# Two additions of the output tail moved to GpSimd, and their stores one step later, in an attention and spectral-mix kernel

## The chip, the cores and the metric

The kernel runs on one core of a Trainium2 chip. The metric is device time in microseconds (us); lower is better. The core's engines run side by side, each with its own instruction queue: TensorE (PE; its weight loads are PEld), VectorE (DVE), ScalarE (ACT), GpSimd (POOL) and SyncE (SP), which here only issues transfers. Sixteen DMA engines move data between HBM and the on-chip memory. TensorE writes its results to PSUM, eight banks of accumulators.

## The reference

Attention with a local mask for half of the heads and a strided mask for the other half gives x, 8 batches of 576 tokens by 512 channels. Then a spectral mix, and an output layer with a residual:

```python
    X = np.fft.rfft(x, axis=1)
    Yr = np.einsum('bmd,mde->bme', Xr, w_r) - np.einsum('bmd,mde->bme', Xi, w_i)
    Yi = np.einsum('bmd,mde->bme', Xr, w_i) + np.einsum('bmd,mde->bme', Xi, w_r)
    y = np.fft.irfft(Y, n=S, axis=1)
    u = x + y
    return (u + np.maximum(u @ w_ch, 0.0)).astype(np.float32)
```

The first 64 frequencies ("modes") are mixed, each with its own two 512 x 512 matrices. What matters for the change is the last line: the output is u = x + y plus the relu of v = u @ w_ch.

## The kernel before, in words

The kernel has three stages. The first computes the attention, batch by batch, and its Fourier transform over the tokens. The second runs over the 64 modes in two halves of the input channels and streams in the weights (fp16 on chip) through GpSimd's DMA queue; the chip works on x @ w_ch and on spectra that are already whole in between. The third, the tail, is where the change lies.

Because the inverse transform is linear, u and v are sums of a part that is known early (x, and x @ w_ch, with the contributions of the first three groups of sixteen modes already added to them by `renew` during the second stage; they are kept in fp16 as `xos`/`xoh` and `v0s`/`v0h`) and the contribution of the last group. The tail adds that last contribution, takes the relu, adds and stores. It runs over 18 items (`items`, from line 973). Items 0 to 15 are 128 tokens of two batches each: 128 partitions by 2 x 512 values in fp32, 512 KB. Items 16 and 17 are the last 64 tokens of four batches each, again 512 KB.

Order of work is written out by hand; each engine runs its instructions in the order in which the program issues them. For each item k the program issues:

- `v_early(k)`, line 984: two matmuls with the identity put the kept v into a pair of PSUM banks (L987);
- `u_early(k)`, line 989: two matmuls with the identity put the kept x into another pair (L992);
- `new_rows(k, ...)`, line 994: two matmuls (four for items 16 and 17) add the last group's rows, once for v from the spectra `zzs`, once for u from `yys` (L1001). They use 32 rows of the array each;
- `v_done(k)`, line 1008: ScalarE writes the relu of v into a tile `rl` (L1013);
- `u_done(k)`, line 1015: VectorE adds u from PSUM and `rl` into the output tile `osb` (L1020), and SyncE issues the store (L1028). For items 16 and 17 four stores of 128 KB go out, two by SyncE and two by ScalarE (L1031).

The loop from line 1065 makes step k of v's first half for item k and the second half of u for item k - 1: in one step TensorE runs `v_early(k)`, `u_early(k-1)`, the rows of v for k, and the rows of u for k - 1; then come ScalarE's relu of k, VectorE's add for k - 1 and its store. Before step 8, four more matmuls (`spec_z(3, 1, held)`) and a ScalarE copy make the spectra `zzs[1]` of the second four batches.

Buffers: PSUM pool "p" has three pairs of banks, taken in turn by v of every item, by u of the even items, and once by `held`; pool "u" has one pair, for u of the odd items. `osb` comes from a pool of five buffers (NWBUF, line 27), so item k takes the buffer of item k - 5 once its store has landed. `rl` has two pairs of buffers.

Of the kernel before, what the change touches and what calls it, by code (L numbers as in the profile page):

```python
# [10 lines left out]
FP = mybir.dt.float32  # L11
F16 = mybir.dt.float16
AluOp = mybir.AluOpType
# [5 lines left out]
DM = 512  # L19
# [37 lines left out]
def kernel(  # L57
# [10 lines left out]
    nc = tc.nc  # L68
# [17 lines left out]
    def psum(kind, half=False, pair=False):  # L86
        if pair:
            return pss[kind].tile([128, 2, 512], FP, tag=kind, name=kind)
        if half:
            return pss[kind].tile([128, 1024], F16, tag=kind, name=kind)  # L90
        return pss[kind].tile([128, 512], FP, tag=kind, name=kind)
# [39 lines left out]
    pw = ctx.enter_context(tc.tile_pool(name="pw", bufs=NWBUF))  # L131
# [118 lines left out]
    def act_copy(out, in_):  # L250
        nc.scalar.activation(out=out, in_=in_, func=ACTF.Copy)  # L251
# [445 lines left out]
    def out_cols(t):  # L697
        if t < 4:
            return ds(256 * (t % 2) + 128 * (t // 2), 128)
        return ds(512, 64)  # L700

    v0s, xos = {}, {}
# [165 lines left out]
    xoh = [ptr.tile([128, DM], F16, name=f"xoh{i}") for i in range(4)]  # L868
    zzs = [ptr.tile([128, DM], F16, name=f"zz{i}") for i in range(B)]
    yys = [ptr.tile([128, DM], F16, name=f"yy{i}") for i in range(B)]  # L870
# [31 lines left out]
    A3 = cs["cFl"].rearrange("p a t m -> p (a t m)")[:, 0:S]  # L902
# [64 lines left out]
    for n, i in enumerate([3, 5, 7] + list(range(8, 21))):  # L967
        b, t = n // 2, n % 2 * 2
# [4 lines left out]
    items = []  # L973
# [6 lines left out]
    def own(item, kept, half):  # L980
        bs, t = item
        return [kept[b][:, t] for b in bs] if t < 4 else [half[b // 2] for b in bs[::2]]

    def v_early(k):
        vps[k] = psum("p", pair=True)
        for j, r in enumerate(own(items[k], v0s, v0h)):
            nc.tensor.matmul(vps[k][:, j], idn, r, start=True, stop=False)  # L987

    def u_early(k):
        ups[k] = psum(("p", "u")[k % 2], pair=True)  # L990
        for j, r in enumerate(own(items[k], xos, xoh)):
            nc.tensor.matmul(ups[k][:, j], idn, r, start=True, stop=False)  # L992

    def new_rows(k, acc, spectra):
        bs, t = items[k]
        for j, b in enumerate(bs):
            q = ds(32 * (b % 4), 32)
            o, cols = acc[:, j % 2], out_cols(t)
            if t == 4:
                o = acc[ds(64 * (b % 2), 64), j // 2]  # L1000
            nc.tensor.matmul(  # L1001
                o, A3[q, cols], spectra[b // 4][q], start=False, stop=True
            )

    def pieces(k):
        return [slice(0, 1), slice(1, 2)] if k == 0 else [slice(0, 2)]

    def v_done(k):
# [3 lines left out]
        for j in pieces(k):  # L1012
            nc.scalar.activation(out=rls[k][:, j], in_=vp[:, j], func=ACTF.Relu)  # L1013

    def u_done(k):
        bs, t = items[k]
        up, rl = ups.pop(k), rls.pop(k)
        osb = pw.tile([128, 2, DM], FP, tag="w", name="osb")
        for j in pieces(k):
            nc.vector.tensor_tensor(  # L1020
                out=osb[:, j], in0=up[:, j], in1=rl[:, j], op=AluOp.add
            )
            if t < 4:
                rows = out[:, ds(128 * (t - t % 2), 256), :].rearrange(
                    "b (p i) e -> p b i e", i=2
                )
                own_b = slice(bs[0] + j.start, bs[0] + j.stop)
                nc.sync.dma_start(rows[:, own_b, t % 2], osb[:, j])  # L1028
        if t == 4:
            for b in bs:  # L1030
                (nc.scalar if b % 2 else nc.sync).dma_start(  # L1031
                    out[b, ds(512, 64), :], osb[ds(64 * (b % 2), 64), b // 2 % 2, :]
                )

    flush()
    rest = [(0, m) for m in range(SPLIT1, NM)] + [(1, m) for m in range(SPLIT0, NM)]
    late[22] = [lambda: v_early(0), lambda: v_early(1), lambda: u_early(0)]
    for i, (slot, m) in enumerate(rest):
        mode(slot, m)
# [16 lines left out]
    for k in range(2):  # L1056
        new_rows(k, vps[k], zzs)
    for k in range(2):
        v_done(k)
    for k in range(2):  # L1060
        if k:
            u_early(k)
        new_rows(k, ups[k], yys)
        u_done(k)
    for k in range(2, LAST + 2):
        if k == 8:
            held = psum("p", pair=True)[:, 0]
            spec_z(3, 1, held)
            act_copy(zzs[1], held)
        if k <= LAST:  # L1070
            v_early(k)
        if k > 2:
            u_early(k - 1)
        if k <= LAST:
            new_rows(k, vps[k], zzs)
        if k > 2:
            new_rows(k - 1, ups[k - 1], yys)
        if k <= LAST:
            v_done(k)
        if k > 2:  # L1080
            u_done(k - 1)
# [31 lines left out]
```

## Time and profile before

| | |
|---|---|
| median of three runs | 428.08 us (427.69 to 428.46) |
| profiled execution: span, first to last instruction | 426.7 us |
| profiled execution: device time of its own | not given by the page |
| busy PE, DVE, ACT, POOL | 346.4, 234.7, 218.3, 110.7 us |
| mean granted TensorE clock | 0.926 |
| data moved by the core's DMA engines | 91.62 MB, mean 215 GB/s |
| written to HBM | 9.44 MB |
| store of an item (512 KB): issues, median time to landing | 15, 3.4 us |

The profile is one execution. Its times are us from the span's start. "L987" is line 987 of the kernel. A line of the timeline gives the start, the duration, the engine, the line, the operation, out<-in with partitions x elements and type, how many, and in brackets how long the engine had been idle and what it waited for. SPq and ACTq are the queues that issue transfers. DMA share is the mean busy share of the sixteen DMA engines. The chain that ended last follows the work back from the last instruction, at each step to what released it.

### The profile page before, as it was taken

What the parts mean: (1) busy time and instruction counts of PE and PEld (TensorE: products, weight loads), DVE (VectorE), ACT (ScalarE), POOL (GpSimd) and SP (SyncE); (2) the same over time, 40 slices, a digit from 0 to 9 for tenths busy, and PEclk for the clock granted to TensorE, in tenths of its full rate; (3) what the DMA queues carried; (4) which work ended last, traced back from release to release, by engine and by line L of the source; (5) the groups of instructions that cost most, each with busy time, mean ns of one, the idle gap of its engine ahead of it and who ended that gap; (6) DMA issues with size and microseconds to landing.
All of it is one profiled execution on the core that took longest, in us unless ns stands there. A gap on an engine that the chain in (4) does not pass through costs nothing.

```text
span 426.7 us, 9768 instructions
## 1 busy us (share of the span) xinstructions
PE 346.4 (81%) x4167; PEld 208.2 (49%) x4167; DVE 234.7 (55%) x466; ACT 218.3 (51%) x390; POOL 110.7 (26%) x196
## 2 busy tenths in 40 slices
PE   2977878769999698889768788878788867889993
PEld 2866767554656365566433344435444423445330
DVE  3788778851355154356113246746676354655884
ACT  1687678643656356556642235423442444443872
POOL 8332333322423222222222322222232222210000
PEclk9999899967999689999995889989999979989997
DMA  8999999999999999999999999999999999995698
GB/s 150 210 212 212 213 213 213 211 211 211 214 213 213 213 213 215 212 214 215 210 214 211 213 214 213 210 213 215 212 213 214 213 213 214 214 212 105 244 355 287
DMA packets 30938, 91.62 MB, mean 215 GB/s; under 512 B 4464, under 2 KB 5232, under 8 KB 30896
## 3 DMA queue, kind: packets, MB, share of 16 engines
q0 software_dynamic: 25168, 81.28, 96.2%
q1 hardware_dynamic: 4976, 9.13, 5.9%
q10 hardware_dynamic: 752, 0.61, 0.5%
q8 instruction: 32, 0.52, 0.5%
q14 instruction: 10, 0.08, 0.0%
HBM read 162.83 MB, written 9.44 MB: 404 GB/s over the span
## 4 chain that ended last, share of the span: by engine, by line
DMA 47%; PE 29%; DVE 14%; ACT 5%; issue 3%; DVEq 0%; POOL 0%; ACTq 0%; POOLq 0%
DMA wt<-in_moe_w_i_dram 38%; DMA wt<-in_moe_w_r_dram 7%; PE y L597 5%; DVE xb L241 3%; DVE kz L283 3%; PE p L987 2%; ACT X L251 2%; PE sc L532 2%; PE tp L413 2%; PE sc L459 1%; PE p L1001 1%; PE y L532 1%; PE p L760 1%; DVE yy L752 1%; DVE rec L240 1%
## 5 line engine op out<-in xcount | busy, mean ns | idle before, releaser
L597 PE MATMUL y<-wt,X 128*32 128x512 f16 (+1 forms) x448 | 70.9, 430 | 20.1 <-DMA wt<-in_moe_w_i_dram 20.1
L186 POOL DMA_DIRECT2D wt<-in_moe_w_r_dram x59 | 34.7, 588 | 126.4 <-PE y L597 56.3
L186 POOL DMA_DIRECT2D wt<-in_moe_w_i_dram x60 | 35.4, 590 | 68.3 <-DMA wt<-in_moe_w_i_dram 44.4
L597 PEld LDWEIGHTS <-X 128*32 128x32 f16 (+1 forms) x448 | 28.1, 140 | 39.4 <-DMA wt<-in_moe_w_i_dram 18.6
L727 DVE COPY xo<-tp 128x512 f16<-128x512 f16 x32 | 22.1, 691 | 36.8 <-PE tp L725 36.8
L726 ACT ACTIVATE v<-sc 128x512 f16<-128x512 f32 x32 | 19.1, 597 | 44.2 <-PE sc L717 44.2
L717 PE MATMUL sc<-w_cp,xT 128*128 128x512 f16 x128 | 36.9, 410 | 1.9 <-DVE xT L690 1.9
L489 ACT ACTIVATE PL<-sc 128x480 f16<-128x480 f32 (+1 forms) x48 | 27.0, 578 | 21.3 <-PE sc L475 21.0
L241 DVE TENSOR_TENSOR xb<-av,rec 90x256 f16<-90x256 f32 (+2 forms) x80 | 36.0, 450 | 2.8
L240 DVE RECIPROCAL rec<-av 90x4 f32<-90x4 f32 (+2 forms) x80 | 14.6, 183 | 39.3 <-PE av L504 28.2
L251 ACT ACTIVATE yr<-y 128x512 f16<-128x512 f32 x28 | 16.7, 597 | 36.8 <-PE y L597 35.6
L961 DVE TENSOR_TENSOR xo<-p,xo 128x1024 f16<-128x1024 f32 x16 | 19.6, 1225 | 21.7 <-PE p L760 21.7
L420 DVE COPY qT<-tp 128x576 f16<-128x576 f16 x16 | 11.9, 752 | 34.7 <-PE tp L413 34.7
L251 ACT ACTIVATE v<-p 128x1024 f16<-128x1024 f32 x16 | 16.4, 1023 | 23.1 <-PE p L760 23.1
L378 ACT ACTIVATE PL<-sc 90x360 f16<-90x360 f32 (+1 forms) x48 | 22.7, 490 | 7.0 <-PE sc L371 6.4
L251 ACT ACTIVATE v<-tp 128x640 f16<-128x640 f16 (+1 forms) x24 | 19.0, 807 | 11.8 <-PE tp L447 9.3
L413 PE MATMUL tp<-cI_s,ring 64*64 64x64 f16 x864 | 22.4, 197 | 2.7 <-DVE qT L420 2.4
L459 PE MATMUL sc<-cMl_s,cI_s 128*128 128x480 f16 (+1 forms) x48 | 19.4, 405 | 4.5 <-ACT PL L489 2.9
L276 PE MATMUL tp<-cI_s,ring 72*128 72x72 f16 x256 | 15.4, 207 | 8.7 <-DMA ring<-in_v_dram 7.1
L413 PEld LDWEIGHTS <-ring 64*64 64x64 f16 x864 | 17.5, 110 | 9.4 <-issue 5.4
L251 ACT ACTIVATE kz<-tp 64x360 f16<-64x360 f16 (+1 forms) x32 | 18.9, 592 | 6.2 <-PE tp L413 5.2
L1013 ACT ACTIVATE rl<-p 128x1024 f32<-128x1024 f32 (+1 forms) x19 | 18.4, 979 | 5.7 <-PE p L1001 3.1
(142 smaller groups left out, 737.9 us busy)
## 6 DMA issues: line engine op xcount, KB each, us to landing
wt<-in_moe_w_i_dram POOLq DMA_DIRECT2D x60, 512.0 KB, 18.8
wt<-in_moe_w_r_dram POOLq DMA_DIRECT2D x59, 512.0 KB, 17.7
out_dram<-osb SPq DMA_DIRECT2D x15, 512.0 KB, 3.4
ring<-in_v_dram POOLq DMA_DIRECT2D x8, 288.0 KB, 13.4
ring<-in_q_dram POOLq DMA_DIRECT2D x8, 288.0 KB, 13.6
ring<-in_k_dram POOLq DMA_DIRECT2D x8, 288.0 KB, 13.1
ring<-in_v_dram POOLq DMA_DIRECT2D x3, 512.0 KB, 14.8
ring<-in_q_dram POOLq DMA_DIRECT2D x3, 512.0 KB, 14.8
```

The lines of the kernel that those rows point to most:

```text
L186: nc.gpsimd.dma_start(dst, rows)
L241: nc.vector.tensor_tensor(out=dst, in0=val.rearrange("p h (q c) -> p h c q", c=4), in1=rec[0:n, 0:pieces] .to_broadcast((n, pieces, 64)) . ...
L251: nc.scalar.activation(out=out, in_=in_, func=ACTF.Copy)
L378: nc.scalar.activation(out=PS[0:n, ds(POFF[t], 4 * n)], in_=scp[0:n, 0 : 4 * n], func=ACTF.Exp, scale=SCALE,)
L413: nc.tensor.transpose(tp[ds(64 * hp, 64), ds(64 * i, 64)], qn[ds(64 * hp, 64), ds(64 * (9 * g + i), 64)], idn[ds(64 * hp, 64), ds(64 * hp, ...
L459: nc.tensor.matmul(scp[:, 0 : n * times].rearrange("p (h x) -> p h x", h=times), idn, mask_rows("cMl", n, times), start=True, stop=False,)
L489: nc.scalar.activation(out=dst, in_=src, func=ACTF.Exp, scale=SCALE)
L597: nc.tensor.matmul(yp[ds(a, 32), :], Xh[half][pr, c].rearrange("p b r (h m) -> p (b r h) m", h=2)[:, :, mm % 32], wt[pr, XC[c], :], start= ...
L717: nc.tensor.matmul(vp, xT[:, ch], w_chs["cp"][:, ch, :], start=(ch == 0), stop=(ch == 3),)
L726: nc.scalar.activation(out=v0, in_=vp, func=ACTF.Copy)
L727: nc.vector.tensor_copy(out=xo.rearrange("p (h q c) -> p h q c", h=2, c=4), in_=tp[:, 0:512].rearrange("p (h c q) -> p h q c", h=2, c=4),)
L961: nc.vector.tensor_tensor(out=xo, in0=up[:, 0:n], in1=xo, op=AluOp.add)
```

## The change

Items 2, 6, 8, 12 and 14 (`XADD`) leave out `u_early`: x isn't put into PSUM by TensorE. The first row matmul opens the accumulation instead (`start=fresh`). VectorE adds the relu as before, and then GpSimd adds x, in two instructions of 128 x 512, from the kept fp16 tile onto the fp32 output tile.

Items 4 and 10 (`RADD`) keep `u_early`, but VectorE's add is left out: ScalarE copies u from PSUM to `osb`, and GpSimd adds the relu in one instruction of 128 x 1024.

The store of these seven items isn't issued in their own `u_done` but in that of the next item, behind that item's own store. The store's code is the same, in a function of its own.

```diff
+    XADD = (2, 6, 8, 12, 14)
+    RADD = (4, 10)
+
     def u_early(k):
         ups[k] = psum(("p", "u")[k % 2], pair=True)
+        if k in XADD:
+            return
         for j, r in enumerate(own(items[k], xos, xoh)):
             nc.tensor.matmul(ups[k][:, j], idn, r, start=True, stop=False)
 
     def new_rows(k, acc, spectra):
         bs, t = items[k]
+        fresh = spectra is yys and k in XADD
...
             nc.tensor.matmul(
-                o, A3[q, cols], spectra[b // 4][q], start=False, stop=True
+                o, A3[q, cols], spectra[b // 4][q], start=fresh, stop=True
             )
...
+    stores = {}
+
+    def store(k):
+        if k not in stores:
+            return
+        osb = stores.pop(k)
...
     def u_done(k):
-        bs, t = items[k]
         up, rl = ups.pop(k), rls.pop(k)
-        osb = pw.tile([128, 2, DM], FP, tag="w", name="osb")
+        osb = stores[k] = pw.tile([128, 2, DM], FP, tag="w", name="osb")
+        if k in RADD:
+            act_copy(osb, up)
+            nc.gpsimd.tensor_tensor(out=osb, in0=osb, in1=rl, op=AluOp.add)
+            return
         for j in pieces(k):
             nc.vector.tensor_tensor(
                 out=osb[:, j], in0=up[:, j], in1=rl[:, j], op=AluOp.add
             )
...
+        if k in XADD:
+            for j, r in enumerate(own(items[k], xos, xoh)):
+                nc.gpsimd.tensor_tensor(out=osb[:, j], in0=osb[:, j], in1=r, op=AluOp.add)
+            return
+        store(k)
+        store(k - 1)
```

## The prediction

> **What bounds the kernel now.** I read the two dies' table first (one core, clock 0.926, 426.7 us), then the page's slices, the chain that ended last, the tail's stretches, and the timeline and DMA issues of the tail. The chain puts 47% of the span on weight loads. They end at 391.6 us; the change lies wholly behind them, in the tail of 18 items from 396.7 us on. There the chain names TensorE:
>
> ```profile
> 414.90 0.43 PE p L992 x2
> 415.33 0.33 PE p L1001 x4
> 415.66 0.54 PE p L987 x2
> 416.20 0.43 PE u L992 x2
> 416.63 0.34 PE p L1001 x4
> ...
> 418.92 0.83 DVE osb L1020
> 419.75 0.08 issue
> 419.83 1.44 DVEq L1108
> ```
>
> A step is 0.54 + 0.43 + 0.33 = 1.30 us of TensorE: two matmuls of v, two of x, four of spectral rows. But the stretches (columns: busy us of PE, PEld, DVE, ACT, POOL; clock, DMA share, GB/s) show a second full resource:
>
> ```profile
> 401.00:408.00 7.00, 6.86 (x42) 2.24 (x42) 5.49 (x5) 5.01 (x7) 0.00 (x0) 1.00 1.00 374
> 408.20:409.00 0.80, 0.80 (x8) 0.20 (x5) 0.80 (x1) 0.74 (x1) 0.00 (x0) 1.00 0.19 72
> 409.00:421.00 12.00, 10.69 (x72) 3.23 (x68) 10.89 (x10) 8.19 (x8) 0.00 (x0) 1.00 1.02 380
> 422.00:425.00 3.00, 0.00 (x0) 0.00 (x0) 0.00 (x0) 0.00 (x0) 0.00 (x0) 0.50 0.88 307
> ```
>
> DMA share is 1.00 and 1.02 at 374 to 380 GB/s. An item is 512 KB, so its store takes 524,288 B / 380 GB/s = 1.38 us, and items come every 1.30 us: the stores are already slower than TensorE. Only the gap around 408.5 us, after the extra matmuls of step 8, lets the queue run dry. The timeline and the issues give the other prices:
>
> ```profile
> 404.16 1.02 ACT L1013 ACTIVATE rl<-p 128x1024 f32<-128x1024 f32 x1 [0.27 <-PE p L1001]
> 404.25 1.23 DVE L1020 TENSOR_TENSOR osb<-p,rl 128x1024 f32<-128x1024 f32 x1
> 405.13 0.60 ACT L251 ACTIVATE zz<-p 128x512 f16<-128x512 f32 x1
> 406.72 1.23 DVE L1020 TENSOR_TENSOR osb<-u,rl 128x1024 f32<-128x1024 f32 x1 [1.24 <-PE u L1001]
> ...
> 420.06 1.22 DVE L1020 TENSOR_TENSOR osb<-u,rl 128x1024 f32<-128x1024 f32 x1
> 420.17 2.44 SPq L1031 DMA_DIRECT2D out_dram<-osb  x4
> ```
>
> ```profile
> 7.19 1.16 POOL L329 COPY PL<-cT_s 128x576 f16<-128x576 f16 x1
> ```
>
> ACT's relu is 1.02 us, VectorE's add 1.23, and GpSimd's one arithmetic row of size is 1.16 us for 576 elements. A store issued at 407.97 has its first packet at 408.86 and has landed 2.8 us after issue: 0.9 to the first packet, 1.38 of data, 0.5 to land.
>
> **Part 1: x leaves TensorE for five items.** Ten L992 matmuls go, 0.43 us a pair: 5 x 0.43 = 2.15 us of TensorE. Taken alone that is the gain, if nothing else bound. The row matmuls that now open the accumulation cost nothing extra: the same four stand in the step. But VectorE still adds relu (1.23 us, with starts at best 1.14 apart: 418.92 to 420.06), so a pair of items falls to 2.3, not 2.17 us, while its stores need 2.76 us. The saved time has nowhere to go.
>
> **Part 2: GpSimd.** Two adds of 512 elements per x item, one of 1024 per relu item; none is in the trace. From below, VectorE's 1.2 ns an element: 1.2 us an item. Nearest, the copy's 2.02 ns an element: 2.1 us. From above, one copy's time for each of the two inputs: 4.1 us. I take 2.25, near the copy row with a little for the second input; up to 2.6 us, two steps, GpSimd keeps up. POOL's queue is otherwise empty: its last weight load is issued at 382.3.
> The Trainium skill (GPSIMD Engine Reference, sections 3.1 and 4.1) speaks against the change: elementwise work belongs on VectorE, GpSimd taking 4497 ns for 2048 fp32 against 2293. By that an item's adds are an estimated 2.25 us; by the copy row they are 2.1, and the end is the same either way.
>
> **Part 3: relu of items 4 and 10.** VectorE loses two adds (2.46 us); ACT gains two 1.02 us copies, each behind the next item's relu. ACT idles 0.27 us a step, so a copy leaves it about 0.75 us late for the next relu; TensorE's buffers absorb part of it. It eats what item 2 saved: the copy of item 4 ends near 403.3, relu 6 near 404.35 (ended at 403.88 before), relu 7 near 405.4, the copy of zz[1] near 406.0, and VectorE adds item 7 at 406.7, as before.
>
> **Part 4: the order of stores.** On SP each of the seven even stores is put behind the odd one: 3, 2, 5, 4, ... 15, 14, and waits there for GpSimd; behind it in SP's queue wait the next pair's stores and, at the end, SP's half of 16 and 17. The number of SP issues (0.37 us each) is unchanged. I walk both kernels by the same prices (issue + 0.9, then 1.38 in order).
>
> Before: item 2 (issue 400.32) starts at 401.22; items 2 to 6 are out at 401.22 + 6.90 = 408.12; item 7 (407.97) starts at 408.87; items 7 to 15 are out at 408.87 + 12.42 = 421.29.
>
> After: item 1 is unchanged. Relu 2 ends at 398.64 (ACT is busy with four relus from 395.53), relu 3 at 399.65; TensorE's step 4 cannot start before 398.64 and ends at 399.95; item 3's add runs 400.0 to 401.24, issue 401.29, first packet 402.19 where item 2's stood at 401.22: the queue loses 0.97 us. Item 3 out 403.57; item 2 (add to 399.95, GpSimd to 402.2) 404.95; item 5 406.33; item 4 (copy to 403.3, GpSimd to 405.6, first packet 406.54) 407.92, 0.21 lost; item 7 (issue 408.01, packet 408.91) 410.29, with item 6, long added by VectorE, behind it: 0.99 lost, where the gap was 0.75 before. Then 6, 9, 8, 11, 10, 13, 12, 15, 14 without gap: 410.29 + 12.42 = 422.71. That is 0.97 + 0.21 + 0.24 = 1.42 us later than 421.29.
>
> **Buffers.** Five output buffers: item k waits for the store of k-5. Item 6, out at 411.67, lands at 412.2, and item 11's add waits 0.5 us for it; that is covered, since its store still arrives (414.4) before 414.43. Item 17 waits for item 12 (419.95 + 0.5): its add runs 420.6 to 421.8, against 421.28 before. Last data came 3.78 us after that add (425.06 - 421.28), so by this path at 425.6.
>
> **The end.** Items 16 and 17 are 1.05 MB. Before they needed 425.06 - 421.29 = 3.77 us, because they came late and in small stores. Now they find a full queue. At best 380 GB/s: 2.76, last data 425.5; at worst 3.77: 426.5. Nearest is the stretch 422 to 425, 307 GB/s at share 0.88, so 349 if never idle: 3.0 us, 425.7. I add 0.2 for the waits on GpSimd that the walk takes as free: 425.9, which is 0.85 us later than 425.06. After it 1.6 us to the span's end stay. Span 426.7 + 0.85 = 427.5. The page gives this execution no device time; the median 428.08 lies 1.4 us above its span, and with that the forecast is 428.9, call it 429.0.
>
> **Rivals.**
> *Stores stay the bound, GpSimd keeps pace* (the forecast): 425.5 to 426.5 gives 428.5 to 429.5; chance 0.60, of it 0.38 above the 428.94 where "slower" begins (0.2%, about what a measurement of this kernel can tell from no change).
> *The end packs better (not slower).* The late 1.05 MB, starved before, runs at 380 GB/s, and the refill after step 8 comes 0.25 us sooner because ACT catches up: 1.42 - 0.25 - 1.01 = +0.16, so 428.2. It decides once the last two items need under 2.9 us. For it: the 0.88 share; against: 128 KB stores never ran over 307 GB/s in that stretch. Chance 0.13.
> *TensorE's saving comes through.* If stores were not the bound, pairs at 2.3 instead of 2.6 give 5 x 0.3 = 1.5 us: 426.6. Against it stands the DMA share of 1.02. Chance 0.04.
> *GpSimd becomes the bound.* At 4.1 us an item, seven items back to back from 400.0 end at 428.7; store 14 then needs 0.05 + 0.9 + 1.38, and 16 and 17 stand behind it: 431.0 + 3.0 = 434.0, +9, 437. At 3.0 us: 400 + 21 = 421.0, store out 423.3, end 426.3 or with buffer waits 426.7: +1.6, 429.7. It decides from 2.6 us an item. Chance 0.15, mostly near 429.7 to 431.
> *A first-use delay or a shared port.* GpSimd's first add may be slow once, or its adds may hold up VectorE. From below 0: the copy at 7.19 follows a memset at 7.14 with no gap, so a known operation starts at once. From above: if each of the 12 adds holds VectorE for its own 1.1 us, 13 us, less GpSimd's own slack; I put the weight at 1 to 4 us: 430 to 433. Chance 0.08.
> The Trainium skill (the same page, section 2.1) gives about 6 us for a first call to freshly loaded code; its page SBUF — State Buffer (Who interferes with whom) says a VectorE add with one SBUF input does not collide with GpSimd. No run here shows either; by the first the sum would be some 4 us higher, by the second the port costs nothing.
>
> **How the numbers follow.** Likeliest 429.0 (own range 428.5 to 429.5). Faster than 427.22: 0.05 (the saving 0.04, and 0.01 of packing). Within 0.2%: 0.22 of the forecast's case + 0.12 of packing = 0.34. Slower: 0.38 + 0.15 + 0.08 = 0.61. Leaving out the saving, the lower half of packing and the worst of GpSimd gives 428.2 to 431.8.
>
> **What would show it.** L992 has ten fewer matmuls in the tail; GpSimd shows twelve adds near 1.1 or 2.25 us; no store between issue 398.8 and about 401.3; DMA idle near 401.5 and again near 408.5; share near 1 from 409 to the end. It is wrong if GpSimd's adds take over 1.3 us per 512 elements, if VectorE's adds grow beyond 1.23 us beside them, or if the stores move over 380 GB/s.

## The result

The changed kernel takes 429.26 us (median of 11 runs, 428.42 to 430.35), the kernel before 428.06 us beside it (11 runs, 427.29 to 429.16). The ratio is 1.0032 with a 95% interval of 1.0023 to 1.0041: slower by 1.4 us (1.2 by the medians), and the whole interval lies above the 0.2% from which the prediction speaks of slower. 429.0 was forecast. Ratios here and below leave out one execution of 584 us, in a slower state, of the kernel with one queue for the merged stores.

The profiled execution has a span of 427.4 us, 0.7 us over the one before and not 1.4. The tail shows why: its first store is issued at 396.20 us, 0.68 us sooner than the 396.88 before. That lies ahead of the change and differs from execution to execution: the weight stream ended at 391.63 us before and 391.22 after, and first stores lie between 395.67 and 396.88 us in these profiles. So tails are compared from their own first store.

Stretches of the tail after the change (columns: busy us of PE, PEld, DVE, ACT, POOL; clock, DMA share, GB/s):

```profile
400.00:402.00 2.00, 2.00 (x15) 0.62 (x14) 0.72 (x1) 1.73 (x3) 1.66 (x2) 1.00 0.42 158
405.00:406.00 1.00, 1.00 (x8) 0.26 (x7) 0.00 (x0) 0.29 (x2) 1.00 (x2) 1.00 0.81 307
407.20:408.20 1.00, 1.00 (x8) 0.29 (x6) 1.00 (x2) 0.71 (x1) 0.12 (x1) 1.00 0.22 82
408.20:421.00 12.80, 10.20 (x68) 3.08 (x64) 9.75 (x9) 8.79 (x9) 9.14 (x7) 1.00 1.02 378
422.00:425.00 3.00, 0.00 (x0) 0.00 (x0) 0.00 (x0) 0.00 (x0) 0.00 (x0) 0.57 0.98 305
```

Before, from item 1 to item 15, the DMA engines were idle only around 408.5 (and for 0.1 us at 401). Now they are short of work in three places: from 400 to 402 (share 0.42), a little at 405 (0.81), and at 407.7, where the old gap was (0.22). From 408.2 on they are as full as before (378 GB/s, 380 before), so what was lost by then is not made up. The last row is the stores of the last two items, at 305 GB/s with the engines full.

The chain that ended last still ends in TensorE and VectorE, and has taken in GpSimd:

```profile
411.80 2.36 POOL osb L1046
414.16 0.02 issue
414.18 1.03 ACT rl L1019
415.22 0.04 issue
415.26 0.59 PE p L987 x2
415.85 0.43 PE u L997 x2
...
418.67 0.73 DVE osb L1049
419.40 0.09 issue
419.49 1.54 DVEq L1132
```

It follows engines; the stores between them don't show in it.

GpSimd's adds, from the timeline:

```profile
399.39 2.27 POOL L1054 TENSOR_TENSOR osb<-osb,xo 128x512 f32<-128x512 f32 x2 [16.97 <-DVE osb L1049]
402.71 2.37 POOL L1046 TENSOR_TENSOR osb<-osb,rl 128x1024 f32<-128x1024 f32 x1 [1.05 <-ACT osb L251]
405.03 2.29 POOL L1054 TENSOR_TENSOR osb<-osb,xo 128x512 f32<-128x512 f32 x2
408.44 2.27 POOL L1054 TENSOR_TENSOR osb<-osb,xo 128x512 f32<-128x512 f32 x2 [1.12 <-DVE osb L1049]
```

An item costs GpSimd 2.27 to 2.37 us, under two steps of 1.30; the first add is as quick as the later ones. The waits of SyncE's queue:

```profile
SPq L1034 <- POOL osb L1046: 2.7, 2, 1.4
SPq L1034 <- POOL osb L1054: 1.6, 3, 0.6
```

SyncE waits 4.3 us in all for GpSimd, for five of the seven late stores.

### The profile page after: what moved, and what is told of

Same layout as the page of the kernel before. It is cut to its first block, busy times and chain, and to the rows that moved or that the text cites. A ratio compares the mean times of both kernels' runs of the same rounds, so it can differ in the third digit from the quotient of the medians.

```text
span 427.4 us, 9775 instructions
## 1 busy us (share of the span) xinstructions
PE 342.8 (80%) x4157; PEld 207.0 (48%) x4157; DVE 232.2 (54%) x464; ACT 219.6 (51%) x392; POOL 127.2 (30%) x208
## 4 chain that ended last, share of the span: by engine, by line
DMA 57%; PE 19%; DVE 12%; ACT 5%; issue 3%; POOL 2%; DVEq 0%; ACTq 0%; POOLq 0%
DMA wt<-in_moe_w_i_dram 45%; DMA wt<-in_moe_w_r_dram 6%; DMA ring<-in_v_dram 4%; PE y L597 3%; DVE xb L241 3%; DVE kz L283 2%; PE sc L532 2%; ACT X L251 2%; DMA ring<-in_q_dram 1%; DVE yy L752 1%; ACT rl L1019 1%; DVE rec L240 1%; PE sc L717 1%; PE av L392 1%; PE tp L276 1%
## 5 line engine op out<-in xcount | busy, mean ns | idle before, releaser
L597 PE MATMUL y<-wt,X 128*32 128x512 f16 (+1 forms) x448 | 68.7, 419 | 22.6 <-DMA wt<-in_moe_w_i_dram 22.5
L532 PEld LDWEIGHTS <-xb 108*128 108x128 f16 (+2 forms) x176 | 15.4, 106 | 11.6 <-DVE xb L241 7.6
```

The lines of the kernel that those rows point to most:

```text
L532: nc.tensor.matmul(xp[:, ds(192 * cp, 192)].rearrange("p (f m) -> p f m", f=3), xb[b][0:n, base + t, ds(128 * cp, 128)], F[0:n, :, t, :], ...
L597: nc.tensor.matmul(yp[ds(a, 32), :], Xh[half][pr, c].rearrange("p b r (h m) -> p (b r h) m", h=2)[:, :, mm % 32], wt[pr, XC[c], :], start= ...
```

## The experiments

The store-queue theory says that the 16 DMA engines set the end, and that the change costs what it leaves them idle, because an even item's store stands behind the odd one's. Its rivals: GpSimd's work itself costs the time (by its duration, or by holding up another engine), or TensorE sets the end, as the chain says. Each ratio is against the kernel before, run beside it. "Out" is when the data of the first 16 items (8 MB) has left, counted from the packet records; "out" and "last data" are us from the tail's first store, each from one profile. Five profiles whose first sixteen items are stored alike (before, adds aside, and three of the kernels further down with other stores at the end) have "out" at 24.57 to 24.65; "last data" repeats less well (28.17 and 28.48 in the two of them that also end alike). The kernel before had medians of 427.70 to 428.15 us beside these kernels.

| kernel | median us | ratio, 95% interval | out | last data |
|---|---|---|---|---|
| before | 428.06 | 1 | 24.60 | 28.17 |
| changed | 429.26 | 1.0032 [1.0023, 1.0041] | 25.98 | 29.52 |
| order alone | 429.30 | 1.0027 [1.0014, 1.0040] | 26.02 | 29.80 |
| stores in their own step | 430.53 | 1.0056 [1.0042, 1.0070] | 27.68 | 31.28 |
| x left out | 427.64 | 0.9992 [0.9982, 1.0003] | 24.37 | 28.02 |
| adds aside | 427.73 | 0.9992 [0.9981, 1.0003] | 24.57 | 28.48 |
| x part only | 428.76 | 1.0019 [1.0007, 1.0031] | 25.44 | 29.16 |
| item 2 late | 428.36 | 1.0004 [0.9995, 1.0013] | 25.15 | 28.71 |
| item 6 late | 429.41 | 1.0031 [1.0019, 1.0042] | 25.97 | 29.61 |

### The order of the stores alone

```diff
-    XADD = (2, 6, 8, 12, 14)
-    RADD = (4, 10)
+    XADD = ()
+    RADD = ()
+    LATE = (2, 4, 6, 8, 10, 12, 14)
...
+        if k in LATE:
+            return
         store(k)
         store(k - 1)
```

> The kernel before in all its arithmetic (TensorE adds x, VectorE adds the relu, GpSimd idle); only the stores of items 2, 4, ... 14 go out one step later, behind the next item's. Store-queue theory (the end is set by the stores, and what the change costs is the stretches in which the DMA engines run dry): the first store after item 1 is that of item 3, issued at 401.62 where item 2's was at 400.32, so the queue loses 1.3 us at the start and about 0.1 more at step 8: +1.4 us, 429.5 us, as slow as the changed kernel without any GpSimd work. GpSimd theory (the adds and ScalarE's copies cost the time): no change, 428.1 us.

429.30 us, as slow as the changed kernel, with no GpSimd add and all of TensorE's matmuls. "Out" is 1.42 us over the kernel before; 1.4 was expected. The cost of the change is in the order of its stores; the rest of it comes out near nothing.

### The stores in their own step

```diff
             act_copy(osb, up)
             nc.gpsimd.tensor_tensor(out=osb, in0=osb, in1=rl, op=AluOp.add)
+            store(k)
             return
...
                 nc.gpsimd.tensor_tensor(out=osb[:, j], in0=osb[:, j], in1=r, op=AluOp.add)
+            store(k)
             return
```

> The changed kernel, but each of the seven even items' stores is issued in its own step, so SyncE waits for GpSimd ahead of the odd item's store. Store-queue theory: item 2's store is issued at about 402.25 instead of 400.32, and the queue dries again at items 4 and 10 (0.6 and 0.8 us): 2.6 us over the kernel before, 430.7 us; the later issue of the even stores is then what spares about 1.2 us in the changed kernel. GpSimd theory: the same work, so the same time as the changed kernel, 429.4 us.

430.53 us, where 430.7 was expected. GpSimd's work is that of the changed kernel; only SyncE's order differs, and it is 1.3 us slower (medians from different sets of runs). Its stretches at the start:

```profile
400.00:403.00 3.00, 3.00 (x20) 0.86 (x19) 1.63 (x2) 2.73 (x4) 1.95 (x3) 1.00 0.30 114
403.00:406.00 3.00, 2.47 (x16) 0.94 (x14) 1.49 (x2) 2.10 (x4) 3.00 (x2) 1.00 0.80 296
```

The DMA engines stand idle for 2.1 us of the first three while SyncE waits for item 2. So with GpSimd in the path the late order is the better of the two; without GpSimd, no lateness is needed.

### TensorE's saving alone

```diff
-    RADD = (4, 10)
+    RADD = ()
...
-        if k in XADD:
-            for j, r in enumerate(own(items[k], xos, xoh)):
-                nc.gpsimd.tensor_tensor(out=osb[:, j], in0=osb[:, j], in1=r, op=AluOp.add)
-            return
```

> TensorE's ten matmuls of x are left out for items 2, 6, 8, 12 and 14 and nobody adds x there (the result lacks x in these items); relus and stores as before, GpSimd idle. Store-queue theory: 2.15 us less of TensorE gives only what fills the dry stretch at step 8 and brings the last add forward, 0.3 to 0.6 us: 427.5 to 427.8 us. TensorE theory (the chain's reading): 1.5 to 2.15 us, 426.0 to 426.6 us.

This kernel leaves x out of the five items altogether. 427.64 us; the interval, 0.9982 to 1.0003, takes in no change and excludes the 1.5 us of the TensorE theory. The last rows of its chain still name TensorE, ScalarE and VectorE:

```profile
412.77 1.01 ACT rl L1019
413.79 0.04 issue
413.83 0.59 PE p L987 x2
414.42 0.43 PE u L997 x2
```

but its stretches name the stores:

```profile
400.00:401.00 1.00, 1.00 (x8) 0.41 (x8) 0.93 (x2) 0.73 (x2) 0.00 (x0) 1.00 0.41 156
402.00:421.00 19.00, 14.93 (x96) 4.66 (x94) 15.41 (x13) 12.33 (x13) 0.00 (x0) 0.98 1.02 373
421.00:424.00 3.00, 0.00 (x0) 0.00 (x0) 0.00 (x0) 0.00 (x0) 0.00 (x0) 0.50 0.87 298
```

The gap of step 8 is gone, TensorE is busy for 14.93 of 19 us, and the engines move 373 GB/s all the way. VectorE's last add ends 23.43 us after the first store, 0.97 sooner than before; the last data comes 0.15 us sooner, less than it varies by itself. In this profile a new gap stands at 400 to 401, 0.9 us after item 2's store was issued; why isn't settled. It takes part of what the faster TensorE gave: item 7's store is issued 10.53 us after the first, 11.09 before, so without that gap the items might be out up to 0.56 us sooner (an estimate from these two), which is still far from 1.5.

### GpSimd's adds aside

```diff
+    side = w_chs["cp"].rearrange("p c e -> p (c e)").bitcast(FP).rearrange("p (j e) -> p j e", j=2)
+
+    def aside(k):
+        rl = rls[k]
+        if k in (4, 10):
+            nc.gpsimd.tensor_tensor(out=side, in0=side, in1=rl, op=AluOp.add)
+        elif k in (2, 6, 8, 12, 14):
+            for j, r in enumerate(own(items[k], xos, xoh)):
+                nc.gpsimd.tensor_tensor(out=side[:, j], in0=side[:, j], in1=r, op=AluOp.add)
...
     def u_done(k):
+        aside(k)
```

> The kernel before, with GpSimd making the changed kernel's twelve adds beside it into a tile that nothing reads. Store-queue theory: VectorE's adds stay at 1.23 us and the stores go out as before: 428.1 us within 0.2%. GpSimd theory (port shared with VectorE, or another contention): VectorE's adds grow where GpSimd runs, over 1.3 us each, and the time rises by 0.5 us or more.

427.73 us, no change. In the tail's groups GpSimd's adds and VectorE's stand beside each other:

```profile
L1031 DVE TENSOR_TENSOR osb<-u,rl 128x1024 f32<-128x1024 f32 x9 | 11.0, 1223 | 2.1 <-PE u L1001 1.6
L1031 DVE TENSOR_TENSOR osb<-p,rl 128x1024 f32<-128x1024 f32 x8 | 9.8, 1224 | 1.0 <-PE p L1001 0.6
L1023 POOL TENSOR_TENSOR w_cp<-w_cp,xo 128x512 f32<-128x512 f32 x8 | 9.0, 1157 | 0.2
L1020 POOL TENSOR_TENSOR w_cp<-w_cp,rl 128x1024 f32<-128x1024 f32 x2 | 4.7, 2371 | 18.0 <-ACT rl L1013 18.0
```

VectorE's add stays at 1.22 us (the two adds of item 2 ran ahead of this stretch). GpSimd doesn't hold it up. The Trainium skill's page SBUF — State Buffer (Who interferes with whom) says so of a VectorE operation with one SBUF input, and the run agrees.

### The x part without the relu part

```diff
-    RADD = (4, 10)
+    RADD = ()
```

> The changed kernel with GpSimd's relu part taken back (items 4 and 10 as before, their stores in order); x of items 2, 6, 8, 12 and 14 stays on GpSimd with the late stores. Store-queue theory: item 3 still goes first after item 1, so the start's loss of about 1.1 us stays; the dry stretch at item 4's late store and the later start of item 7, which ScalarE's copies cost, go, about 0.7 us less than the changed kernel: 428.7 us. If the relu part cost nothing, as a theory that looks at the start alone would have it: 429.4 us.

428.76 us, where 428.7 was expected; "out" is 0.54 us under the changed kernel's (the two medians come from different sets of runs, and their intervals overlap). The place where it shows is item 7's store: issued 11.09 us after the first store before, 10.53 with the x part alone, 11.06 in the changed kernel. TensorE's saving brings it forward by 0.56 us, and the relu part takes 0.53 back. In the changed kernel's timeline TensorE's extra matmuls of step 8 wait for a relu that stands behind ScalarE's copy, and item 7's add comes after them:

```profile
402.52 1.95 ACT L1019 ACTIVATE rl<-p 128x1024 f32<-128x1024 f32 x2
403.60 1.02 PE L736 MATMUL p<-w_ch,YT 128*128 128x512 f16 x4 [0.53 <-ACT rl L1019]
406.01 1.23 DVE L1049 TENSOR_TENSOR osb<-u,rl 128x1024 f32<-128x1024 f32 x1 [1.20 <-PE u L1007]
```

### One late store: item 2, or item 6

```diff
-    LATE = (2, 4, 6, 8, 10, 12, 14)
+    LATE = (2,)
```

> The kernel before with one store late: item 2's goes out behind item 3's; all the rest as before. Where does the queue's loss arise? By the walk through the store queue item 3 starts at 402.52 in place of item 2 at 401.22 (1.3 us lost), items 2 to 6 are out at 409.42, and item 7, whose first packet can come at 408.87, then finds no dry queue: the 0.75 us that the queue was dry at step 8 anyway is given back. 1.30 - 0.75 = +0.55 us: 428.5 us. If a loss at the start simply stays to the end: +1.3 us, 429.2 us.

The other kernel has `LATE = (6,)`.

> The kernel before with one store late: item 6's goes out behind item 7's. By the walk, items 2 to 5 are out at 406.74 and nothing is queued until item 7's first packet at 408.87: the queue is dry for 2.13 us instead of 0.75 us, +1.38 us: 429.3 us, as much as all seven late stores together cost. If the losses add up store by store: a seventh of 1.3 us, 0.2 us, no measurable change.

Item 6 late: 429.41 us. One late store costs as much as all seven. Item 2 late: 1.0004, an interval that takes in no change and, at its edge, the 0.55 us expected; in the profile "out" is 0.55 us later, which is what the walk gave. Two stretches of the kernel with item 2 late,

```profile
400.63:402.23 1.60, 1.60 (x10) 0.41 (x8) 1.53 (x2) 1.33 (x2) 0.00 (x0) 1.00 0.25 93
407.23:409.23 2.00, 2.00 (x15) 0.66 (x15) 1.85 (x3) 1.45 (x3) 0.00 (x0) 1.00 1.03 383
```

and three of the kernel with item 6 late:

```profile
406.00:407.00 1.00, 1.00 (x8) 0.31 (x4) 0.69 (x1) 0.79 (x1) 0.00 (x0) 1.00 0.68 250
407.00:408.00 1.00, 1.00 (x8) 0.41 (x8) 0.93 (x2) 0.73 (x2) 0.00 (x0) 1.00 0.03 10
408.00:409.00 1.00, 1.00 (x9) 0.29 (x7) 0.93 (x2) 0.73 (x2) 0.00 (x0) 1.00 0.55 209
```

With item 2 late the queue idles 1.2 us at the start (share 0.25 of 1.6 us), but at step 8 it is full (1.03), since the work it missed is still queued there: 0.6 of the 1.2 us is given back in the gap that was there anyway. With item 6 late nothing is queued at step 8: item 7 waits for the extra matmuls, and item 6, long ready, waits behind item 7. The three rows leave 1.7 us idle, against 0.65 us around step 8 before, and nothing later gives it back.

The packet records show what the late kernels share. Item 7's first packet comes 11.98 us after the first store before, 11.97 with the order alone, 11.98 with item 6 late and 11.95 in the changed kernel, and in all four the queue is all but empty just ahead of it. From there nine items (7 to 15) have to go out before, ten in the others, since item 6 stands behind item 7. One item's data is 1.38 us, and "out" differs by 1.37 to 1.42. What was lost earlier only shortens the empty stretch at step 8. With the x part alone the queue is empty there too, item 7's first packet comes 0.54 us sooner (11.41), and "out" is 0.54 us below the changed kernel's.

### The last two items

The forecast had reckoned with 3.0 us for the last 1.05 MB; both profiles show 3.5 to 3.6. Five kernels bear on it.

```diff
-            for b in bs:
-                (nc.scalar if b % 2 else nc.sync).dma_start(
-                    out[b, ds(512, 64), :], osb[ds(64 * (b % 2), 64), b // 2 % 2, :]
-                )
+            for par, eng in enumerate((nc.sync, nc.scalar)):
+                eng.dma_start(
+                    out[bs[0] + par : bs[0] + 4 : 2, ds(512, 64), :].rearrange("b p e -> p b e"),
+                    osb[ds(64 * par, 64)],
+                )
```

> The kernel before, with the eight stores of 128 KB of items 16 and 17 made into four of 256 KB (one by SyncE and one by ScalarE for each item). This asks why the last 1.05 MB took 3.5 us in both profiles, at about 305 GB/s with the DMA engines full, and not 2.8 to 3.0. If the small stores are the reason (their number, or the late issue of the last of them): 0.4 to 0.7 us faster than the kernel before, 427.4 to 427.7 us. If the rate goes with two queues at work or with 64 partitions a store: no change, 428.0 us.

The second has `enumerate((nc.sync, nc.sync))`.

> As the kernel with four stores of 256 KB for the last two items, but all four issued by SyncE, so that one queue feeds the DMA engines. If two queues at once lower the rate: back to 370 to 380 GB/s over the last stretch, 2.8 us for the last 1.05 MB, and faster than with two queues. If not: the same as with two queues, or slower by the 0.6 us that one issue waits for the other.

Ratios 1.0009 [0.9999, 1.0020] and 1.0013 [0.9999, 1.0026]: no gain. The last 1.05 MB took 4.27 and 4.19 us, longer than with eight stores, and one queue was no better than two. So neither the number of stores nor the second queue makes the stretch slow. The mean packet of it took 117 and 115 ns, against 88 ns of the 128-partition stores in the same profiles, and 100 ns with the eight stores.

The third is the first, with item 1 made in halves:

```diff
-        return [slice(0, 1), slice(1, 2)] if k == 0 else [slice(0, 2)]
+        return [slice(0, 1), slice(1, 2)] if k < 2 else [slice(0, 2)]
```

> The kernel before with the four stores of 256 KB for the last two items, and with item 1 made in two halves (relu, add and store by batch) as item 0 is. The queue was dry for about 0.45 us before item 1's store; a half store comes some 0.5 us sooner and fills that. Store-queue theory: 0.3 to 0.5 us less than with the four stores alone, at best 427.0 us. If the end goes by VectorE's last add instead: no gain from the split.

1.0015 [1.0004, 1.0026]: no gain over the four stores alone. The gap before item 1 went, and a new one opened from 400.0 to 401.0 (DMA share 0.16): item 2's store was issued 3.50 us after the first, 3.44 before, and the queue had emptied sooner.

The fourth and fifth read all 128 partitions in each of the four stores:

```diff
+            for j, eng in enumerate((nc.sync, nc.scalar)):
+                eng.dma_start(
+                    out[bs[2 * j] : bs[2 * j] + 2, ds(512, 64), :],
+                    osb[:, j],
+                )
```

> The kernel before, with the last two items stored by four stores of 256 KB that each read all 128 partitions (two batches of one half of the output tile, SyncE and ScalarE one each) in place of eight that read 64 partitions. With the four stores of 64 partitions the packets took 115 ns against 88 ns of the 128-partition stores, and the last 1.05 MB 4.2 us. If the 64 partitions are the reason for the slow last stretch: packets back to about 88 ns, the last 1.05 MB in 2.8 to 3.1 us instead of 3.6, 0.4 to 0.8 us faster than the kernel before, 427.2 to 427.6 us. If it is the destination rows or the lateness of the last issue: 3.6 us and 428.0 us.

> The changed kernel with the same four stores of 128 partitions for the last two items. Store-queue theory: the dry stretches cost what they cost, about 1.4 us over the kernel before with the same last stores; with a last stretch of 2.8 to 3.1 us that is 428.6 to 429.0 us, now what the prediction had reckoned with for the end. If the backlog had been hidden by the slow last stores, the two kernels would come closer than 1 us.

446.53 and 447.26 us, 1.0440 [1.0426, 1.0455] and 1.0458 [1.0443, 1.0472]: both expectations missed, by 18 to 19 us. The stretch says why (kernel before with these stores):

```profile
426.00:442.00 16.00, 0.00 (x0) 0.00 (x0) 0.00 (x0) 0.00 (x0) 0.00 (x0) 0.50 0.13 51
```

Share 0.13 is two of sixteen engines. The destination's outer dimension is the two batches, and the four stores together kept two engines busy. The Trainium skill's page DMA: Bandwidth & Descriptors (Why a DMA increments its semaphore by 16 and not by 1) states it: a transfer is shared by the largest number of engines, up to 16, that divides the slowest dimension of both sides, here 2. The packets themselves took 84 ns there, as the 64-partition reading would have it, but with two engines at work that proves little. The page SBUF — State Buffer (Door 1: The DMA port swizzle) says that 64 partitions reach only half of the ports; the 115 ns packets fit it, and no run here isolates it. With the end stretched so, the changed kernel is still 0.7 us slower by the medians, though the intervals overlap.

No kernel here that computes the whole output beats the kernel before.

## Why the prediction was right

**The bound.** It was read from the DMA share of 1.02 against a chain that names TensorE. Right: with 2.15 us of TensorE's work gone, the medians fell by 0.35 us, and the interval can't tell that from no change.

**The walk through the store queue.** Forecast: the first 16 items out 1.42 us later, of it 0.97 at the start, 0.21 at item 4 and 0.24 at step 8. Measured: 1.38 us (25.98 against 24.60). The places are right: item 3's store was issued 4.55 us after the first store, item 2's before at 3.44, 1.11 later; at 405 to 406 the share of 0.81 is 0.19 us; item 7's store was issued 11.06 us after the first (11.13 forecast, 11.09 before). But the three losses are not the parts of the cost, as the sum suggests: item 6's late store alone gives 1.37, item 2's alone 0.55. The walk's own numbers say what the packets show: item 7's first packet at 408.91 against 408.87, 0.04 us, and behind it one item more, 1.38.

**GpSimd.** 2.25 us an item was taken; 2.27 and 2.37 were measured. No slow first use, no hold on VectorE (1.22 us), so those rivals fall. The GPSIMD Engine Reference's estimate of 2.25 (section 3.1) was nearer than the copy row's 2.1, and it made no difference, as said.

**ScalarE.** Its copies ate TensorE's gain by step 8, as forecast: relu 7 ends 8.3 us after the first store in both profiles, and the copy of zz[1] starts at 8.5 us against 8.3. One wait was not foreseen: relu 14 takes the buffer that GpSimd reads in its add of item 10. The chain after the change shows it, the add from 411.80 to 414.16 and the relu at 414.18; ScalarE waited 0.7 us. It cost nothing, since the store queue had work.

**Buffers.** Item 17's add was forecast at 23.7 us after the first store for want of item 12's buffer; it came at 23.61, and ended 24.83. The nearness is luck: the add started 1.14 us after item 16's, directly behind it, and the chain leads from there over TensorE back to the relu 14 that waited for GpSimd, not to a store. That add was not what set the end either: last data followed 4.69 us after it.

**The step that failed** is the last one, "Now they find a full queue": 3.0 us for the last 1.05 MB against 3.77 before, a gain of 0.77 against which 0.2 was set for waits. Measured, it was 3.54 against 3.58: no gain. The walk's own starting figure, 3.77, was 0.2 high since it ran its queue 0.2 ahead of the data. About half of what a full queue was to win is slower packets: 512 of 100 ns are 3.2 us on sixteen engines, of 88 ns 2.8. The 349 GB/s came from reading the 0.88 share of the stretch before as waiting; after the change the share is 0.98 and the rate still 305 GB/s. Why the packets are slower stays open. Without that gain the forecast would have been 0.85 + 0.57 = 1.42 us, 429.5; the measured ratio gives 1.37. The range held because its upper end had been worked out without that gain.

The rival in which the end packs better falls with the same finding, and the one in which TensorE's saving comes through with the run that leaves x out.

## What to carry to other kernels

Look for a resource that is full beside the one that the chain names: here the chain followed engines, and the DMA share in short stretches showed that the stores were already slower than TensorE. In a queue that is served in order, what a late entry costs is the time the server then stands empty, minus the gaps further on that would have been there anyway; walk the queue, don't add up delays. A ready transfer must not stand behind one that is still waiting: one such store, ahead of a step known to be slow, cost as much as all seven.

## What was not expected of the hardware

The stores that read 64 partitions moved 305 GB/s at a DMA share of 0.98, where those of 128 moved 378 at 1.02, and their packets of 2 KB took 100 to 117 ns on average against 88 ns. Stores whose destination has an outer dimension of two used two of the sixteen engines: 51 GB/s, and 19 us more.
